# Blockwise causal attention and a gated FFN on one core: moving the casting loads of batches 4 to 7, and batch 3's key and query copies, within the order of issue

## The chip, the cores and the metric
One core of a Trainium2 chip runs the whole program as one launch. The metric is the device time of an execution in microseconds (us). PE, ACT, DVE, POOL and SP are the core's engines: matmul, activation, vector, GpSimd and the engine that issues most transfers. A line of the form "L266" is line 266 of the kernel file.

## The reference
The input is q, k and v of 8 batches, 8 heads, 576 positions and 64 dimensions in float32, and three weights. Cut to what matters:

```python
scores = (q @ k.T) / sqrt(64)                   # per batch and head
scores = where(pos_q // 64 >= pos_k // 64, scores, -1e9)
attn   = softmax(scores)                        # float32
x      = (attn @ v) -> [4608 tokens, 512]       # heads side by side
out    = (relu(x @ w_gate) * (x @ w_val)) @ w_out   # 512 -> 1536 -> 512
```

## The kernel before, in words
**Tiles.** The FFN works on nine tiles j of 512 tokens. Tile j, for j from 0 to 7, holds the first 512 positions of batch j; the ninth tile holds the last 64 positions of all eight batches. One tile is 144 matmuls: 12 blocks f of d_ff, each four for the gate and four for the value (L615), and then four output blocks of 12 (L634). `ffn_gen` yields after each of them, so the kernel counts in *places*: place p of a tile is its p-th FFN matmul, and places 0 to 95 are gate and value, 96 to 143 the outputs.

**Attention between the FFN matmuls.** While tile b-1 runs, the attention of batch b is laid between its matmuls: four rounds r = 4b to 4b+3, one for each pair of heads hp = 0 to 3, and one "tail" for the last 64 queries. A round begins with `visit` (L426, scores from `kTm` and `qTm` of its hp), goes on with exponentials on ACT (L435, L441), zeroed corners on DVE (L495), two `head_av` (L553, then L507 and L508 on DVE, which write `xnat`), and ends with `to_xT_dma` (L583), a transposing transfer issued by SP that writes one quarter of `xT`, the operand of FFN tile b. Tile b can't run the fourth matmul of its first block before the fourth quarter of its `xT` has landed. The tail is `tail_visit` (L460, reads `kTm`, all hp), `tail_av` (L522, reads `v_bf`) and L536.

**Order.** The order on every engine is written by hand: `run(base, events)` sorts (place, function) pairs and calls each function after so many FFN matmuls. Each engine goes through its own list in that order and waits there only for the data and buffers of the next instruction. So a place fixes what stands before what on an engine; a transfer whose inputs and buffer are free may be issued long before the FFN reaches that place.

**How q, k and v come in.** Batches 0 to 3 are loaded as float32 into `stage` by SP and cast on POOL or DVE. For batches 2 and 3 the main parts of q and k are transposed by SP into `perm` (L252, one transfer for each of q and k and half hg = hp // 2), and `unpermute` puts them in order: for each hp a copy of 128x512 into `qTm` on DVE and one into `kTm` on POOL, both L266. `v_3` casts batch 3's v on POOL (L203, L217); it writes `v_bf` of the batches with odd number and so waits for the tail of batch 1. Batches 4 to 7 are loaded by `load_qkv` (L316), transfers that POOL issues and that cast on the way: five for each of q, k and v. SP then transposes q and k straight into `qTm`, `kTm`, `qTt`, `kTt` (`dma_transposes`, L326 and L330). All buffers `qTm`, `kTm`, `qTt`, `kTt`, `v_bf`, and `q_bf`, `k_bf`, exist twice, for even and odd batches. So v of batch b+1 can only be loaded once the tail of batch b-1 is through, and q and k of batch b+2 only once those of batch b have been transposed.

**Around the change.** Tile 1 (base 144) runs batch 2, tile 2 (base 288, `b == 3` in the last loop) runs batch 3 with its rounds 12 to 15 at places 2, 26, 74 and 96, and the tail of batch 2 at places 50, 69 and 73. Written `un(3, hp, (dve, pool))`, batch 3's copies stand at place 124 of tile 1 (hp 0) and places 11, 35 and 83 of tile 2 (hp 1 to 3); the loads of q and k of batch 4 stand at place 1 of tile 2.

```python
264  def unpermute(self, hp, engs):
265      for t in range(2):
266          engs[t]((qTm, kTm)[t]..., self.perm[t, hp // 2]...)
304  def load_qkv(b, which):
305      for t in which:
307          for c in range(NCH):          # NCH = 5
316              nc.gpsimd.dma_start(dst, src...)
```

Of the kernel before, what the change touches and what calls it, by code (L numbers as in the profile page):

```python
# [17 lines left out]
def kernel(  # L18
# [12 lines left out]
    B, H, S, D = q.shape  # L31
# [78 lines left out]
    def new_bf():  # L110
        return [sb.tile([128, 2048], BF, name=n, bufs=2) for n in ("q_bf", "k_bf")]

    def new_bt():
        return [sb.tile([64, 512], BF, name=n, bufs=2) for n in ("q_bt", "k_bt")]
# [189 lines left out]
    def load_qkv(b, which):  # L304
        for t in which:
            src = (q, k, v)[t]
            for c in range(NCH):
                n = 128 if c < 4 else 64
                if t == 2:
                    dst = v_bf[b % 2][:n, c, :, 0:64]  # L310
                else:
                    if (b, 0) not in bfs:
                        bfs[b, 0], bfs[b, 1] = new_bf(), new_bt()
                    dst = bfs[b, 0][t][:, 512 * c : 512 * c + 512] if c < 4 else bfs[b, 1][t]
                    dst = dst.rearrange("p (h d) -> p h d", h=8)
                nc.gpsimd.dma_start(  # L316
                    dst,
                    src[b, :, 128 * c : 128 * c + n, :].rearrange("h p d -> p h d"),
                )
# [3 lines left out]
    def dma_transposes(b):  # L323
        m, tl = bfs[b, 0], bfs[b, 1]
        for t in range(2):
            nc.sync.dma_start_transpose(  # L326
                (qTm, kTm)[t][b % 2].rearrange("p c h n -> p (c h) n"),
                m[t],
            )
            nc.sync.dma_start_transpose((qTt, kTt)[t][b % 2][:, 0:4, :], tl[t])  # L330
# [337 lines left out]
    dve, act, pool = nc.vector.tensor_copy, nc.scalar.copy, nc.gpsimd.tensor_copy  # L668
    with tc.manual_schedule(engines={E.PE, E.DVE, E.Activation, E.Pool, E.SP}):
# [89 lines left out]
        def run(base, events):  # L759
            for p, f in sorted(events, key=lambda e: e[0]):  # L760
                upto(base + p)
                f()

        def round_at(p, r, av, to_xT, late=(), corner_eng=None):

            exps = []

            def begin():
                exps.extend(visit(r))
                exps[0]()  # L770
                exps[1]()

            return [
                (p, begin),
                (p + 6, lambda: exps[2]()),
                (p + 13, lambda: corners(r, corner_eng or nc.vector)),
                (av[0], lambda: head_av(r, 0)),
                (av[1], lambda: head_av(r, 1)),
                (to_xT[0], lambda: to_xT[1](r)),
            ]  # L780

        def tail_at(p, b, av):
            exps = []
            x = sb.tile([64, 512], BF, name="xtail", bufs=2)

            def begin():
                exps.extend(tail_visit(b))
                exps[0]()
                exps[1]()

            def end():
                tail_av(b, 1, x)
                tail_to_xT(b, x)

            return [
                (p, begin),
                (p + 6, lambda: exps[2]()),
                (av[0], lambda: tail_av(b, 0, x)),
                (av[1], end),
            ]  # L800
# [53 lines left out]
        def un(b, hp, engs=(dve, dve)):  # L854
            return lambda: early[b].unpermute(hp, engs)

        events = []
# [12 lines left out]
        events = tail_at(4, 0, (20, 24)) + tail_at(116, 1, (132, 136))  # L870
        for r, p in ((8, 32), (9, 52), (10, 72), (11, 92)):
# [12 lines left out]
            (82, lambda: mains_3(4)),  # L884
            (101, lambda: early[3].transpose(1)),
            (118, lambda: early[3].transpose_tails()),
            (124, un(3, 0, (dve, pool))),
            (137, v_3),
        ]
        run(144, events)  # L890
        for b in range(3, B):
            events = tail_at(120, b, (136, 140))
            if b == 3:
                events += tail_at(50, 2, (69, 73))
                events.append((1, lambda: load_qkv(4, (0, 1))))
            for i, p in enumerate((2, 26, 74, 96) if b == 3 else (2, 32, 62, 92)):
                r = 4 * b + i
                events += round_at(p, r, (p + 20, p + 24), (p + 24, to_xT_dma))
                if b == 3 and i < 3:
                    events.append((p + 9, un(3, i + 1, (dve, pool))))  # L900
            if b + 1 < B:
                events.append((75 if b == 3 else 28, lambda b=b: load_qkv(b + 1, (2,))))
                events.append((60, lambda b=b: dma_transposes(b + 1)))
            if b + 2 < B:
                events.append((100 if b == 3 else 59, lambda b=b: load_qkv(b + 2, (0, 1))))
            run(144 * (b - 1), events)
        ffn(10**6)
        store.pop()()
# [28 lines left out]
```

## Time and profile before
| | |
|---|---|
| median of 11 runs | 380.26 us (377.51 to 383.24) |
| the profiled execution's own time | 376.65 us |
| its span, first to last instruction | 374.9 us |
| outside the span | 1.75 us |
| PE busy | 358.7 us, 96% of the span |
| DVE, ACT, POOL busy | 169.2, 171.2, 118.9 us |
| granted TensorE clock | 1.000 |
| moved by POOL's casting loads | 8.13 MB, 56576 packets |

The span is what the views of the profile divide. PE is not busy for 16.2 us of it. The windows view gives PE's busy time for each stretch of the span; the waits view says what PE waited for; the timeline of POOL says what was issued ahead of it.

### The profile page before, as it was taken

The numbers are of one execution on the slowest core, as the hardware profiler recorded it, in microseconds if no ns is written. First come the engines' busy times: TensorE is split into PE (matmuls) and PEld (weight loads), VectorE is DVE, ScalarE is ACT, GpSimd is POOL, SyncE is SP. The second block draws the span as 40 slices with busy tenths as digits, with TensorE's granted clock in tenths as the row PEclk, the third lists the DMA queues.
The fourth block names the chain that finished last, engine by engine and source line by source line (L and its number), as shares of the span: only waits on it lengthen the run. The fifth ranks groups of instructions, "written<-read, shape, count | busy, mean of one in ns | idle before, by whom it ended". The sixth has DMA issues, their size and how long they took to land.

```text
span 374.9 us, 7560 instructions
## 1 busy us (share of the span) xinstructions
PE 358.7 (96%) x3004; PEld 177.3 (47%) x3004; DVE 169.2 (45%) x392; ACT 171.2 (46%) x283; POOL 118.9 (32%) x156
## 2 busy tenths in 40 slices
PE   7898979999996999899999999999999999999995
PEld 2644444544553545454554455444544454444443
DVE  3644455556543564355335552554345444323432
ACT  4923744576533563455545534653366423302310
POOL 5678767346167086480058003000000000000000
PEclk9999999999999999999999999999999999999999
DMA  8999999969989299999689965945200130020014
GB/s 255 293 370 356 373 185 297 205 170 246 189 129 124 56 126 145 172 130 146 152 95 131 123 125 95 62 79 135 77 16 17 42 100 7 2 84 28 3 35 105
DMA packets 140739, 51.35 MB, mean 137 GB/s; under 512 B 120352, under 2 KB 133920, under 8 KB 140704
## 3 DMA queue, kind: packets, MB, share of 16 engines
q0 software_dynamic: 56576, 8.13, 43.2%
q1 hardware_dynamic: 79424, 34.62, 42.3%
q10 hardware_dynamic: 4704, 8.13, 6.6%
q8 instruction: 23, 0.38, 0.4%
q14 instruction: 12, 0.10, 0.1%
HBM read 37.75 MB, written 9.44 MB: 126 GB/s over the span
## 4 chain that ended last, share of the span: by engine, by line
PE 64%; DMA 2%; DVE 1%; POOL 1%; ACT 0%; issue 0%
PE ffnp L615 36%; PE ffnp L634 18%; PE ffnp L553 3%; DMA xT<-xnat 2%; PE sc L426 2%; PE ffnp L522 2%; PE one L426 1%; PE sc L460 1%; DVE hT L628 0%; PE one L460 0%; POOL kTm L266 0%; POOL k_bf L316 0%; DVE qTm L266 0%; POOL k_bt L316 0%; ACT gate_sb L624 0%
## 5 line engine op out<-in xcount | busy, mean ns | idle before, releaser
L628 DVE TENSOR_TENSOR hT<-gate_sb,ffnp 128x512 bf16<-128x512 bf16 x108 | 74.2, 687 | 100.8 <-PE ffnp L615 80.5
L624 ACT ACTIVATE gate_sb<-ffnp 128x512 bf16<-128x512 f32 x108 | 65.0, 602 | 101.6 <-PE ffnp L615 101.5
L615 PE MATMUL ffnp<-xT,wg 128*128 128x512 bf16 x384 | 102.1, 379 | 1.1 <-DMA xT<-xnat 1.1
L615 PE MATMUL ffnp<-xT,wv 128*128 128x512 bf16 x384 | 102.1, 379 | 0.3 <-ACT gate_sb L624 0.2
L634 PE MATMUL ffnp<-wo,hT 128*128 128x512 bf16 (+1 forms) x444 | 102.3, 373 | 0.0
L615 PEld LDWEIGHTS <-wv 128*128 128x128 bf16 x432 | 40.1, 98 | 47.4 <-issue 4.1
L615 PEld LDWEIGHTS <-wg 128*128 128x128 bf16 x432 | 40.0, 98 | 46.5 <-issue 3.2
L634 PEld LDWEIGHTS <-hT 128*128 128x128 bf16 x444 | 40.2, 98 | 40.0 <-issue 0.8
L435 ACT ACTIVATE attnT<-sc 128x1024 bf16<-128x1024 f32 x56 | 56.9, 1040 | 0.0
L644 DVE COPY ob<-ffnp 128x512 f32<-128x512 f32 (+1 forms) x37 | 25.1, 677 | 41.1 <-PE ffnp L634 41.1
L316 POOL DMA_DIRECT2D v_bf<-in_v_dram x20 | 16.8, 856 | 66.7 <-PE ffnp L522 51.7
L553 PEld LDWEIGHTS <-attnT 128*128 128x128 bf16 x640 | 26.3, 98 | 15.1 <-DVE xnat L508 4.4
L507 DVE RECIPROCAL recip<-ffnp 128x4 f32<-128x4 f32 (+1 forms) x76 | 13.6, 179 | 36.8 <-PE ffnp L553 26.4
L441 ACT ACTIVATE attnT<-one 128x256 bf16<-128x256 f32 x28 | 10.7, 383 | 38.9 <-PE ffnp L426 26.8
L553 PE MATMUL ffnp<-v_bf,attnT 128*128 128x65 bf16 x600 | 28.2, 194 | 0.1
L508 DVE TENSOR_TENSOR xnat<-ffnp,recip 128x256 bf16<-128x256 f32 x60 | 25.5, 424 | 2.1
L426 PEld LDWEIGHTS <-kTm 64*128 64x128 bf16 x224 | 8.7, 94 | 18.4 <-issue 10.6
L426 PE MATMUL sc<-qTm,kTm 64*128 64x512 bf16 (+1 forms) x168 | 16.7, 305 | 0.0
L481 ACT ACTIVATE attnTt<-one 64x256 bf16<-64x256 f32 x8 | 3.0, 376 | 28.0 <-PE ffnp L460 28.0
L472 ACT ACTIVATE attnTt<-sc 128x1024 bf16<-128x1024 f32 x16 | 15.6, 1015 | 0.0
L316 POOL DMA_DIRECT2D k_bf<-in_k_dram x16 | 14.1, 896 | 3.2 <-DMA v_bf<-in_v_dram 3.2
L316 POOL DMA_DIRECT2D q_bf<-in_q_dram x16 | 14.4, 923 | 1.5 <-DMA k_bf<-in_k_dram 1.5
(88 smaller groups left out, 261.1 us busy)
## 6 DMA issues: line engine op xcount, KB each, us to landing
out_dram<-ob ACTq DMA_DIRECT2D x28, 256.0 KB, 2.3
stage<-in_moe_w_gate_dram SPq DMA_DIRECT2D x6, 512.0 KB, 9.3
stage<-in_moe_w_val_dram SPq DMA_DIRECT2D x6, 512.0 KB, 9.5
stage<-in_q_dram SPq DMA_DIRECT2D x6, 512.0 KB, 7.0
stage<-in_k_dram SPq DMA_DIRECT2D x6, 512.0 KB, 7.9
stage<-in_moe_w_out_dram SPq DMA_DIRECT2D x6, 512.0 KB, 9.2
stage<-in_v_dram SPq DMA_DIRECT2D x8, 256.0 KB, 7.1
q_bf<-in_q_dram POOLq DMA_DIRECT2D x16, 128.0 KB, 6.4
```

Source lines behind the costliest of these rows:

```text
L316: nc.gpsimd.dma_start(dst, src[b, :, 128 * c : 128 * c + n, :].rearrange("h p d -> p h d"),)
L426: nc.tensor.matmul(where[c].rearrange("p (c n) -> p c n", n=128), kTm[b % 2][head_of(hh), c, hp, :], qTm[b % 2][head_of(hh), c:4, hp, :], ...
L435: return lambda: nc.scalar.activation(at[:, :, lo : lo + 512], sc, AF.Exp, scale=scale)
L472: return lambda: nc.scalar.activation(at[:, :, 2 * i : 2 * i + 2, 0:256], main[i].rearrange("p g (h n) -> p g h n", h=2), AF.Exp, scale=scale,
L507: nc.vector.reciprocal(recip, av[:, :, 64])
L508: nc.vector.tensor_tensor(out=out, in0=av[:, :, 0:64], in1=recip.to_broadcast([rows, n, 64]), op=AX.mult,)
L553: nc.tensor.matmul(av[:, p, :], at[:, hh, col : col + 128], vb[:, c, h, :], start=(p == 0), stop=(c == p), skip_group_check=True,)
L615: nc.tensor.matmul((gate, val)[t], (wg, wv)[t][i][:, c, fo : fo + 128], x[:, c], start=(c == 0), stop=(c == 3),)
L624: nc.scalar.activation(gate_sb, gate, AF.Relu)
L628: nc.vector.tensor_tensor(out=h, in0=gate_sb, in1=val, op=AX.mult)
L634: nc.tensor.matmul(op, hT[f][:, 128 * s : 128 * (s + 1)], wo[f // 4][:, f % 4, n0:n1], start=(f == 0), stop=(f == 11),)
L644: nc.vector.tensor_copy(ob, op)
```

## The change
- `un(3, 0)` moves from place 124 to 121 of tile 1, and `un(3, 1)` from place 11 of tile 2 to place 125 of tile 1, so both stand ahead of `v_3` (place 137).
- `un(3, 2)` moves from place 35 to place 3 of tile 2, and `un(3, 3)` from place 83 to place 33.
- `load_qkv` of q and k: for batch 4 from place 1 to place 4 of tile 2, so behind `un(3, 2)`. For batch 5 from place 100 of tile 2 to place 4 of tile 3; for batches 6 and 7 from place 59 of the tile before to place 4 of the tile in which the batch before them runs.
- `load_qkv` of v: from place 28 to place 46 for batches 5 to 7; it stays at place 75 for batch 4.
- `dma_transposes` moves from place 60 to 66 in every tile.

```diff
-            (124, un(3, 0, (dve, pool))),
+            (121, un(3, 0, (dve, pool))),
+            (125, un(3, 1, (dve, pool))),
             (137, v_3),
         ]
         run(144, events)
...
             events = tail_at(120, b, (136, 140))
             if b == 3:
                 events += tail_at(50, 2, (69, 73))
-                events.append((1, lambda: load_qkv(4, (0, 1))))
             for i, p in enumerate((2, 26, 74, 96) if b == 3 else (2, 32, 62, 92)):
                 r = 4 * b + i
                 events += round_at(p, r, (p + 20, p + 24), (p + 24, to_xT_dma))
-                if b == 3 and i < 3:
-                    events.append((p + 9, un(3, i + 1, (dve, pool))))
+            if b == 3:
+                events.append((3, un(3, 2, (dve, pool))))
+                events.append((33, un(3, 3, (dve, pool))))
             if b + 1 < B:
-                events.append((75 if b == 3 else 28, lambda b=b: load_qkv(b + 1, (2,))))
-                events.append((60, lambda b=b: dma_transposes(b + 1)))
-            if b + 2 < B:
-                events.append((100 if b == 3 else 59, lambda b=b: load_qkv(b + 2, (0, 1))))
+                for at, which in ((4, (0, 1)), (75 if b == 3 else 46, (2,))):
+                    events.append((at, lambda b=b, w=which: load_qkv(b + 1, w)))
+                events.append((66, lambda b=b: dma_transposes(b + 1)))
             run(144 * (b - 1), events)
```

## The prediction
> **What bounds the kernel now.** I read the page's head, then PE's waits, then the windows of 10 us, then the timelines of POOL, PE and DVE where PE stands still, and last the chain at the tile boundary.
>
> ```profile
> span 374.9 us, 7560 instructions
> PE 358.7 (96%) x3004; PEld 177.3 (47%) x3004; DVE 169.2 (45%) x392; ACT 171.2 (46%) x283; POOL 118.9 (32%) x156
> ...
> PE one L426 <- POOL kTm L266: 3.5, 1, 3.5
> ...
> PE ffnp L615 <- DMA xT<-xnat: 1.1, 1, 1.1
> ...
> 110.00:120.00 10.00, 6.53 (x53) 3.17 (x52) 3.99 (x10) 3.93 (x8) 9.70 (x11) 1.00 2.04 113
> 120.00:130.00 10.00, 10.00 (x102) 5.07 (x100) 5.38 (x12) 6.75 (x11) 0.00 (x0) 1.00 0.59 46
> 130.00:140.00 10.00, 9.90 (x108) 5.09 (x106) 5.73 (x13) 5.77 (x11) 7.22 (x9) 1.00 1.80 143
> ...
> 150.00:160.00 10.00, 8.90 (x82) 4.45 (x79) 3.74 (x10) 4.28 (x7) 4.91 (x6) 1.00 2.00 170
> ```
>
> PE is busy for 96% of the span. After 60 us the windows (busy PE is the second number) show only three holes: 3.47 us in 110 to 120, 0.10 in 130 to 140 and 1.10 in 150 to 160; all others are at 9.96 or more. The first is one single wait of PE for a key copy on POOL, the third one wait for the last quarter of an `xT`. Of the other 11.5 us of idle PE, 7.6 lie before 60 us and 3.9 behind the last matmul, where the change moves nothing. Now what stood on POOL ahead of that key copy (start, duration, instruction, idle time before it and what ended that):
>
> ```profile
> 100.37 1.08 POOL L266 COPY kTm<-perm 128x512 bf16<-128x512 bf16 x1 [9.36 <-PE sc L460]
> 106.50 2.03 POOL L203 CAST v_bf<-stage 128x1024 bf16<-128x1024 f32 x2 [5.05 <-PE ffnp L522]
> 108.47 0.61 POOL L217 CAST v_bf<-stage 64x512 bf16<-64x512 f32 x1
> 109.03 3.75 POOL L316 DMA_DIRECT2D q_bf<-in_q_dram  x4
> ...
> 116.91 0.75 POOL L316 DMA_DIRECT2D k_bt<-in_k_dram  x1
> 117.59 2.11 POOL L266 COPY kTm<-perm 128x512 bf16<-128x512 bf16 x2
> 132.78 4.19 POOL L316 DMA_DIRECT2D v_bf<-in_v_dram  x5 [13.08 <-issue]
> 136.93 1.11 POOL L266 COPY kTm<-perm 128x512 bf16<-128x512 bf16 x1
> 137.94 3.54 POOL L316 DMA_DIRECT2D q_bf<-in_q_dram  x4
> ```
>
> And PE at that time:
>
> ```profile
> 114.80 0.48 PE L553 MATMUL ffnp<-v_bf,attnT 128*128 128x65 bf16 x10
> 118.76 0.28 PE L426 MATMUL one<-qTm,kTm 64*128 64x256 bf16 x1 [3.47 <-POOL kTm L266]
> ```
>
> Batch 3's v casts end at 109.1, then POOL issues the ten loads of q4 and k4 (109.03 to 117.66, 8.6 us), and only then the key copy of hp 1 (117.6 to 118.7). Round 13, at place 26, wanted it when PE was through at 115.29. It got it at 118.76. The copy's own inputs had long been there: its `perm` was written for hp 0 as well, which was copied at 100.37.
>
> **The change part by part.** The instruction orders of the two programs are the same on PE, ACT and SP; they differ on POOL and DVE only in where batch 3's eight copies stand.
>
> *Key copies on POOL.* New order: hp 0, hp 1, v casts, hp 2, q4/k4, hp 3, v4, q5/k5. With the durations above: hp 0 at 100.37 to 101.45; hp 1 at 101.45 to 102.5 (its buffer is freed by the same tail scores, L460, as that of hp 0); the v casts still wait for L522 and run from 106.50 to 109.08, since 4 us of POOL's 5.05 us wait are left over; hp 2 from 109.08 to 110.15; q4/k4 from 110.15 to 118.8; hp 3 to 119.9. Round 13 finds its keys 12.8 us early. PE's 3.47 us go.
>
> *What is late next at round 13.* Besides keys, round 13 needs banks of PSUM. Its second piece (the "ffnp" one) takes one that DVE frees: by 115.34 block 2's product (L628, 114.66 + 0.68) and by 114.74 the first `xnat` of round 12 are through; PE gets there at 115.29 + 0.12 = 115.41. Its first big piece needs the exponential L435 that ended at 110.57. So at most 0.1 us takes the place of the wait. If PE's tail were paced by DVE's second `xnat` instead (115.54 + 0.42 = 115.96), 0.55 us would be left; I take 0 and keep 0.55.
>
> *Query copies on DVE.* The same four copies of 0.59 to 0.60 us move to places where DVE is idle: hp 0 and hp 1 at 102.5 to 103.7 (next on DVE is an `ob` copy at 104.49), hp 2 at about 109.0 (DVE then idles until 111.09, waiting for ACT's gate), hp 3 into the slot that hp 2 had at 121.84, which opens 3.47 us earlier. The `perm` transfers for hp 2 and 3 are issued by SP at 99.32 and 100.68 and these transfers took 3.2 to 4.8 us to land, so by 105.5: 3.5 us before either copy. What leaves is this:
>
> ```profile
> 121.84 0.59 DVE L266 COPY qTm<-perm 128x512 bf16<-128x512 bf16 x1
> ...
> 135.53 1.06 DVE L266 COPY qTm<-perm 128x512 bf16<-128x512 bf16 x1
> 137.01 0.69 DVE L628 TENSOR_TENSOR hT<-gate_sb,ffnp 128x512 bf16<-128x512 bf16 x1
> ```
>
> The copy at 135.53, beside POOL's v4 loads, took 1.06 us, held up the next product, and PE's hole of 0.10 us before 137.75 follows from it. In the new order hp 3 lands beside the k4 loads (118.4), so the long form and the 0.10 us may just move there: 0 to 0.1 gained, I take 0.
>
> [...] The change puts DVE's and POOL's copies of hp 2 side by side at 109.05, and one query copy among k4's loads. The rows say less: POOL's 32 wide q and k load issues took 876 to 1102 ns, also those beside the DVE copy at 111.70 (0.60 us); of four query copies beside POOL work one was longer, by 0.46 us, and beside another a cast on POOL took 1.46 us where its like took 1.04. By the rows the price is 0 to 0.46 us on either engine. [...]
>
> *Loads of batch 4.* 1.1 us later on POOL, one key copy in front. In before they landed 3.3 to 6.5 us after issue; k4's last is now issued at about 118.8 and lands by 125.3. SP's transposes of k4 come at 132.70 - 3.47 = 129.2, those of q4 at 124.8 with q landed by about 121. Cost 0; with 6 us less cover SP would pass the delay to the `xT` quarters behind.
>
> *Loads of batches 5 to 7 and the transposes.* Their places in the text move by up to 90, but on POOL everything from v4 on has the same neighbours (v4, q5/k5, v5, q6/k6, ...), except hp 3's copy, and the same buffers to wait for. v5's first issue at 152.23 waited for tail 3's L522, v6's and v7's for 22.6 and 25.9 us for the same line: POOL runs ahead up to a buffer, and the place doesn't hold it. SP's order is unchanged too. So "none in the last third of a tile" doesn't come about in time: q5/k5 are still issued as soon as v4 is. Cost 0, gain 0.
>
> *The next boundary.* Where the 3.47 us could be lost again:
>
> ```profile
> 146.55 0.43 DVE xnat L508
> 147.00 8.14 DMA xT<-xnat
> 155.18 4.26 PE ffnp L615 x19
> ```
>
> The last quarter of `xT` for tile 3 takes 8.14 us to land, against 2.4 to 2.6 us for transposes in quiet stretches (126.9, 209, 224), because it runs among q5/k5 (k5's issues took 11.9 to 13.5 us to land). PE wants it at 154.08 and waits 1.10. All here hangs on PE: tail 2's L522 releases v4, v4 is followed by q5/k5, round 15 releases the transpose. So it all shifts by 3.47 us, and as hp 3's copy no longer stands between v4 and q5, q5/k5 start up to 1.0 us earlier relative to it. [...] The rows speak for less: k5's issues waited for v4's loads to land (0.88 and 0.84 us of idle POOL at 143.5 and 145.2), and that landing isn't moved. Between 0 and 1.0 I take 0.4.
>
> *Sum against the profiled execution.* 3.47 + 0 + 0.4 = 3.87 us: span 374.9 to 371.0, time 376.65 to 372.8. That execution is 3.6 us below the median of the runs shown, below the fastest even; the wait removed comes from POOL's order alone, not from a landing, so I carry it over unchanged: 380.26 - 3.87 = 376.4. The unknowns give 2.9 (0.55 left at round 13, nothing at the boundary) to 4.6 (1.0 and 0.1 more): 375.7 to 377.4. A measurement of this kernel can tell about 0.5%, 1.9 us, from no change.
>
> **The rivals.**
> - *The boundary eats it (same).* If the transfers from 128 to 155 us are a fixed amount of work at a full rate that doesn't begin earlier, the last `xT` quarter lands at 155.1 whenever it is issued, PE waits up to 1.10 + 3.47 us there, and the time stays at 380.3; half of that gives 378.5. For it: landings of 8 to 13.5 us. Against: 120 to 130 us moved only 46 GB/s, POOL stood idle for 13.08 us until v4 was released by PE. The stretch starts on PE's signal.
> - *Batch 5's loads catch the transpose (slower).* Starting 1.0 us earlier they may stand wholly in front of round 15's transpose instead of partly behind it. Its landing decides: up to 8.14 + 3.47 = 11.6 us there is still a gain. At 13.5 us, the longest landing of a k5 load, PE loses 5.4 more: 380.26 + 1.9 = 382.2. Against: the longest landing of any `xT` transpose there is 9.6 us (round 14).
> - *The executions differ from the profile (faster still).* With 3.6 us between profile and median, there may be a longer wait at the same place in most runs, up to 3.6 more: 372.8 to 375.7.
> - *It doesn't do what it says.* For the loads of batches 5 to 7 that is my forecast already; for the key copies it can't be, as their order on POOL does change.
>
> **How the numbers follow.** Forecast 0.74 (375.7 to 377.4), faster still 0.05, boundary 0.13 (378.0 to 380.5; a fifth of it still over 0.5% faster), slower 0.08 (over 380.5; a quarter of it within 0.5%). That makes faster 0.79 + 0.03 = 0.82; I take off 0.03 as the median itself moves by about 1 us from set to set: 0.79. Same 0.14, slower 0.07. The range reaches from 374.0, half of the faster rest, to 379.6, most of the boundary case.
>
> **What would show it.** Right: no wait of PE for `kTm` L266; window 110 to 120 full; POOL with two key copies before the v casts and one on either side of the q4/k4 loads; L426 of round 13 at about 115.3; the loads from v4 on at their old distance from PE's tail scores; a wait at tile 3's first block between 0.1 and 1.1 us. Wrong: that wait at 3 us or more (boundary), landings of over 11.6 us (slower), PE waiting at round 13 for DVE, or q6/k6 issued only when PE reaches tile 4, which would mean that places do hold POOL.

## The result and the profile after

The changed kernel takes 373.72 us (median of 12, 371.61 to 377.72), against 379.46 us for the kernel before (47 runs in all). The ratio is 0.9858, 95% interval 0.9831 to 0.9886: about 5.4 us, 4.3 to 6.4 by the interval. Comparisons and the means further down leave out executions more than 1.5% above the fastest of the same kernel in their set of runs. The forecast was 376.4 us in a range of 374.0 to 379.6, from a gain of 3.87 us. It started from a median before of 380.26 us, and from there the ratio gives 374.9 us; the measured median itself lies 0.3 us below the range. Faster was right; the gain is about 1.5 us larger than the sum, and the experiments look for these 1.5 us.

The profiled execution after has almost the span of the one before. The page's head, PE's waits and the windows of 10 us (the second number is busy PE, the last three are the granted clock, that is the share of its full clock that PE was given, the transfers' share and GB/s):

```profile
span 374.5 us, 7561 instructions
...
PE ffnp L615 <- DMA xT<-xnat: 1.6, 1, 1.6
...
10.00:20.00 10.00, 7.86 (x116) 5.57 (x114) 6.05 (x17) 7.62 (x12) 5.90 (x16) 0.83 1.03 293
...
50.00:60.00 10.00, 9.45 (x86) 4.75 (x87) 3.20 (x9) 5.16 (x9) 7.39 (x11) 0.83 1.03 252
...
110.00:120.00 10.00, 10.00 (x73) 4.71 (x72) 5.74 (x11) 5.80 (x11) 10.00 (x13) 1.00 1.12 76
120.00:130.00 10.00, 9.90 (x114) 5.30 (x113) 5.46 (x12) 6.38 (x11) 2.48 (x3) 1.00 1.22 101
...
150.00:160.00 10.00, 8.44 (x70) 4.06 (x68) 3.70 (x11) 4.28 (x7) 4.72 (x6) 1.00 2.25 164
```

No wait for a key copy is left among PE's waits, and 110 to 120 us is full. But twice before 60 us, where nothing was changed, the clock fell (0.83 over 10 us), and round 12 starts at 111.29 us instead of 108.62. So two spans compare badly; stages compare well. Here is POOL's list and PE's rounds 12 to 15 and the next boundary, all of after:

```profile
103.04 2.10 POOL L266 COPY kTm<-perm 128x512 bf16<-128x512 bf16 x2 [12.29 <-PE sc L460]
109.18 2.03 POOL L203 CAST v_bf<-stage 128x1024 bf16<-128x1024 f32 x2 [4.03 <-PE ffnp L522]
...
111.71 1.06 POOL L266 COPY kTm<-perm 128x512 bf16<-128x512 bf16 x1
112.72 3.64 POOL L316 DMA_DIRECT2D q_bf<-in_q_dram  x4
...
120.47 0.77 POOL L316 DMA_DIRECT2D k_bt<-in_k_dram  x1
121.15 1.33 POOL L266 COPY kTm<-perm 128x512 bf16<-128x512 bf16 x1
132.22 4.19 POOL L316 DMA_DIRECT2D v_bf<-in_v_dram  x5 [9.74 <-issue]
136.37 3.55 POOL L316 DMA_DIRECT2D q_bf<-in_q_dram  x4
```

```profile
111.29 0.28 PE L426 MATMUL one<-qTm,kTm 64*128 64x256 bf16 x1
...
117.89 0.28 PE L426 MATMUL one<-qTm,kTm 64*128 64x256 bf16 x1
...
131.96 0.28 PE L426 MATMUL one<-qTm,kTm 64*128 64x256 bf16 x1
...
137.76 0.28 PE L426 MATMUL one<-qTm,kTm 64*128 64x256 bf16 x1
...
154.83 0.38 PE L615 MATMUL ffnp<-xT,wg 128*128 128x512 bf16 x1 [1.56 <-DMA xT<-xnat]
```

POOL's order is the forecast one. From such first matmuls of the rounds, each stage's length in us (the third column is a later profile of the same changed kernel):

| stage | before | after | after, again |
|---|---|---|---|
| round 12 to 13 | 10.14 | 6.60 | 6.60 |
| round 13 to 14 | 13.75 | 14.07 | 14.06 |
| round 14 to 15 | 6.07 | 5.80 | 5.81 |
| round 15 to 16 | 14.47 | 14.47 | 14.47 |
| round 16 to the end of the span | 221.85 | 222.27 | 221.43 |
| sum | 266.28 | 263.21 | 262.37 |

The wait of 3.5 us is gone in full and the stages behind it gain or lose a few tenths. In all that is 3.1 to 3.9 us, which fits the forecast sum but not the 5.4 us of the times.

### The profile page after: what moved, and what is told of

Its sections match the earlier page's. It is cut to its first block, busy times and chain, and to the rows that moved or that the text cites. A ratio compares the mean times of both kernels' runs of the same rounds, so it can differ in the third digit from the quotient of the medians.

```text
span 374.5 us, 7561 instructions
## 1 busy us (share of the span) xinstructions
PE 360.6 (96%) x3004; PEld 179.0 (48%) x3004; DVE 172.4 (46%) x392; ACT 171.4 (46%) x283; POOL 118.2 (32%) x156
## 4 chain that ended last, share of the span: by engine, by line
PE 88%; DMA 7%; DVE 1%; POOL 1%; issue 1%; SPq 1%; ACT 0%; DVEq 0%; POOLq 0%
PE ffnp L615 49%; PE ffnp L634 24%; PE ffnp L553 5%; PE sc L426 3%; DMA stage<-in_k_dram 3%; DMA xT<-xnat 2%; PE ffnp L522 2%; DMA stage<-in_q_dram 2%; PE one L426 1%; PE sc L460 1%; SPq L132 1%; DVE hT L628 1%; PE ffnp L281 1%; PE ffnp L573 1%; PE sc L375 0%
```

## The experiments

**The parts of the change apart.** First, the copies alone; every load stays at its old place:

```diff
-            (124, un(3, 0, (dve, pool))),
+            (121, un(3, 0, (dve, pool))),
+            (125, un(3, 1, (dve, pool))),
...
-                events.append((1, lambda: load_qkv(4, (0, 1))))
+                events.append((4, lambda: load_qkv(4, (0, 1))))
+                events.append((3, un(3, 2, (dve, pool))))
+                events.append((33, un(3, 3, (dve, pool))))
...
-                if b == 3 and i < 3:
-                    events.append((p + 9, un(3, i + 1, (dve, pool))))
```

> Before with batch 3's eight copies moved as in the change, and every load and transpose left at its old place. If a place in the text doesn't hold POOL (the forecast), this gives the whole of the change: 0.9858, that is about 5.4 us off, like the changed kernel. If the loads' new places carry the part of the gain that the forecast's sum (3.9 us) lacks, about 1.5 us are missing here: 0.990. In the trace: no wait of PE for a key copy of round 13, and POOL's loads of v5, q6/k6 and later at the same distance from PE's tails as in the changed kernel.

Measured: 374.74 us, ratio 0.9874 (0.982 to 0.9929). The copies are the whole change, within the interval.

Second, the loads and transposes alone:

```diff
-                events.append((1, lambda: load_qkv(4, (0, 1))))
...
             if b + 1 < B:
-                events.append((75 if b == 3 else 28, lambda b=b: load_qkv(b + 1, (2,))))
-                events.append((60, lambda b=b: dma_transposes(b + 1)))
-            if b + 2 < B:
-                events.append((100 if b == 3 else 59, lambda b=b: load_qkv(b + 2, (0, 1))))
+                for at, which in ((4, (0, 1)), (75 if b == 3 else 46, (2,))):
+                    events.append((at, lambda b=b, w=which: load_qkv(b + 1, w)))
+                events.append((66, lambda b=b: dma_transposes(b + 1)))
```

> Before with only the loads and the transposes at their new places, the copies left at theirs. Forecast: nothing, ratio 1.000 within 0.3%, PE still waits 3.5 us for the key copy at round 13, and the tile boundary behind round 15 is as before (PE waits about 1.1 us for the last quarter of xT). Rival, that spreading the loads is what pays: 1.5 to 5 us off, 0.987 to 0.996, and q5/k5 issued at least 5 us later against PE's tail 3.

Measured: 378.03 us, ratio 0.9984 (0.9947 to 1.0021). No effect, as forecast: the places don't hold POOL, and the distance of the loads to PE's tails is the same before and after (ahead of v6, POOL waits 22.6 us for L522 in both profiles). In this profile q6/k6 stay where they were, far ahead of tile 4's FFN: POOL is through with them by 170 us and idle from there to 190. But the same trace showed what the profile of before had not. The windows view, 2 us each:

```profile
116.00:118.00 2.00, 0.00 (x0) 0.00 (x0) 0.28 (x1) 0.00 (x0) 2.00 (x4) 1.00 2.13 140
118.00:120.00 2.00, 0.92 (x10) 0.46 (x11) 0.00 (x0) 0.54 (x3) 2.00 (x2) 0.99 3.30 147
120.00:122.00 2.00, 2.00 (x6) 0.70 (x5) 0.00 (x0) 2.00 (x4) 0.02 (x1) 0.50 2.94 96
122.00:124.00 2.00, 2.00 (x7) 0.76 (x6) 1.50 (x4) 0.65 (x2) 0.00 (x0) 0.66 0.12 7
124.00:126.00 2.00, 2.00 (x18) 1.04 (x17) 0.69 (x1) 0.87 (x2) 0.00 (x0) 1.00 0.00 0
```

PE's wait ends at 119.08. About 1 us later the granted clock is 0.50 for some 3.4 us. PE is shown busy, but its matmuls take longer: four FFN matmuls there last 1.91 us, against 1.03 us at the same place in the profile of before. Round 13 to 14 took 15.44 us here, against 13.75: 1.69 us more, 0.45% of the span. So the wait can cost more than its own length. This gives the clock theory, which the next experiments test: the missing 1.5 us is this stretch, which most executions of before have behind round 13 and the profiled one happened not to have.

Third, hp 1's copies alone (hp 2 stays behind q4/k4, hp 3 behind v4):

```diff
             (124, un(3, 0, (dve, pool))),
+            (125, un(3, 1, (dve, pool))),
...
-                if b == 3 and i < 3:
+                if b == 3 and i in (1, 2):
```

> Before with one copy pair moved, that of hp 1 (ahead of the v casts); hp 2 stays behind the q4/k4 loads, hp 3 behind the v4 loads. If round 13's wait is all of it: 3.5 us off at least, and as much as the whole change, 0.986. If in most executions round 15's key copy behind v4 is late too (in the profile of before it ended 0.54 us before its use), or if hp 3's copy ahead of q5/k5 costs at the boundary, part is missing: 3.5 us only, 0.991, and the trace shows PE waiting for kTm at round 15 or the hole of 0.1 us there, or a longer wait at tile 3's first block.

Measured: 374.18 us, ratio 0.9856 (0.9804 to 0.9908): as much as the whole change. Hp 2's and hp 3's copies do nothing that could be measured, and the idea that hp 3's place costs at round 15 or at the boundary has no support in the times. The only profile is of an execution of 381.27 us; no time is read from it. But it shows the boundary and the clock once more (PE's wait, then windows of 1 us):

```profile
PE ffnp L615 <- DMA xT<-xnat: 3.5, 2, 2.0
...
158.00:159.00 1.00, 0.85 (x3) 0.29 (x3) 0.00 (x0) 0.17 (x1) 0.71 (x1) 0.52 2.45 192
159.00:160.00 1.00, 1.00 (x4) 0.40 (x3) 0.00 (x0) 1.00 (x2) 0.64 (x1) 0.50 1.99 102
```

Here the last quarter of `xT` took 10.6 us to land, and PE stood still for 2.01 and 1.45 us with one matmul between, until 158.15. From 158.0 to 160, where these windows end, the clock is 0.50 to 0.52. So the half clock also follows idle PE at another place, with no late key. Why the landing was so long is not shown.

**The clock theory.** The wait kept, but filled: 14 matmuls in front of round 13, whose result nobody reads.

```diff
                 r = 4 * b + i
+                if b == 3 and i == 1:
+                    events.append((p, lambda: junk(14)))
                 events += round_at(p, r, (p + 20, p + 24), (p + 24, to_xT_dma))
```

> Before, with 14 matmuls of 128x512 into an unused bank put on PE right in front of round 13 (they work on v's copy, nothing reads their result): PE is busy for about 3.0 of the 3.5 us in which it waits for hp 1's key copy, and the wait itself stays. Clock theory (the wait of 3.5 us is often followed by a stretch of about 3.4 us at half the granted clock, as the trace of the loads-only kernel shows once, worth 1.7 us): the mean granted clock of the runs rises from about 0.991 to 0.995, as with the changed kernel, and 1.0 to 1.7 us come off, ratio 0.9955 to 0.997. Theory of the sum alone (the wait costs 3.5 us and nothing else): ratio 1.000 or a little above, clock as before.

Measured: 376.61 us, ratio 0.9951 (0.9916 to 0.9986). PE's timeline and the windows:

```profile
115.45 3.18 PE L664 MATMUL ffnp<-v_p,ident 128*128 128x512 bf16 x14
118.83 0.28 PE L426 MATMUL one<-qTm,kTm 64*128 64x256 bf16 x1 [0.20 <-POOL kTm L266]
...
118.00:120.00 2.00, 1.80 (x14) 0.70 (x13) 0.00 (x0) 0.80 (x3) 1.77 (x2) 1.00 2.66 131
120.00:122.00 2.00, 2.00 (x11) 0.90 (x10) 0.70 (x2) 2.00 (x3) 0.00 (x0) 1.00 1.53 99
```

Round 13 starts as late as before (10.16 us after round 12), work was only added, and the kernel is faster by 0.5 to 3.2 us. The sum alone can't give that. The mean granted clock of its runs is 0.9956, against 0.9914 for before in the same set. The idle PE is the cause, not the late key.

The wait shortened: two k4 loads go behind hp 1's key copy.

```diff
-    def load_qkv(b, which):
+    def load_qkv(b, which, cs=range(NCH)):
...
-                events.append((1, lambda: load_qkv(4, (0, 1))))
+                events.append((1, lambda: load_qkv(4, (0,))))
+                events.append((1, lambda: load_qkv(4, (1,), range(3))))
+                events.append((12, lambda: load_qkv(4, (1,), range(3, NCH))))
```

> Before with the last two k4 loads (0.87 and 0.69 us of POOL) moved behind hp 1's key copy: the wait at round 13 shrinks from 3.5 to about 1.9 us. Sum alone: 1.6 us off, ratio 0.996. Clock theory: a wait that short doesn't bring the clock down, so the half-clock stretch goes too: 2.6 to 3.3 us off, ratio 0.991 to 0.993, and the runs' mean granted clock is that of the changed kernel, about 0.995.

Measured: 376.20 us, ratio 0.994 (0.9904 to 0.9977), 2.3 us off by the ratio. That lies between the two forecasts, and the interval holds both. The clock theory's expectation was wrong in one thing: in the profiled execution the shorter wait did bring the clock down:

```profile
117.38 0.28 PE L426 MATMUL one<-qTm,kTm 64*128 64x256 bf16 x1 [1.92 <-POOL kTm L266]
...
118.00:120.00 2.00, 2.00 (x9) 0.73 (x6) 0.00 (x0) 2.00 (x5) 1.87 (x3) 0.50 2.20 149
120.00:122.00 2.00, 2.00 (x8) 0.75 (x7) 0.98 (x2) 0.76 (x1) 0.00 (x0) 0.69 1.50 92
```

So 1.92 us of idle PE can be enough, though on the mean (below) these runs lose no more by the clock than those without a wait.

The wait restored in the changed kernel, and longer, as hp 2's copy stays ahead of q4/k4:

```diff
-            (125, un(3, 1, (dve, pool))),
...
                 events.append((3, un(3, 2, (dve, pool))))
+                events.append((5, un(3, 1, (dve, pool))))
```

> The changed kernel with hp 1's copies put back behind the q4/k4 loads (hp 2 stays ahead of them): PE waits for the key copy at round 13 for 3.5 us plus the 1.05 us of hp 2's copy, about 4.5 us. Sum alone: 4.5 us above the changed kernel, 378.2 us, ratio to before 0.997. Clock theory: such a wait brings the half-clock stretch in nearly every execution, 1.5 to 1.7 us more: 379.8 us, ratio 1.000 to 1.002, and a mean granted clock of about 0.990. If something else in the change carried the gain, the time stays near 374.

Measured: 380.49 us, ratio 1.0049 (1.001 to 1.0088): 6.8 us above the changed kernel by the medians, for a wait of 4.38 us. The sum alone (0.997) lies outside the interval; the clock theory's 1.000 to 1.002 reaches just into it and was itself too low.

```profile
121.95 0.28 PE L426 MATMUL one<-qTm,kTm 64*128 64x256 bf16 x1 [4.38 <-POOL kTm L266]
...
122.00:124.00 2.00, 2.00 (x12) 0.75 (x13) 0.00 (x0) 1.67 (x4) 0.89 (x1) 0.61 2.38 150
124.00:126.00 2.00, 2.00 (x7) 0.73 (x6) 0.46 (x1) 1.31 (x2) 0.00 (x0) 0.53 0.02 1
```

**All runs by their clock.** Every execution has a mean granted clock. Span times (1 - clock) is what it lost by a lower clock, and one stretch of 3.4 us at half clock is 1.7 us of it. A mean clock says how much an execution lost, not where; where is seen in profiles alone. Means over the executions compared (for the runs of before in the first comparison no clock is on record):

| PE at round 13 | executions | mean clock | lost, us | of them under 0.9925 |
|---|---|---|---|---|
| waits 3.5 us (before, three sets) | 50 | 0.9910 | 3.40 | 32 |
| waits 3.5 us (loads only) | 10 | 0.9922 | 2.94 | 4 |
| waits 3.5 us (v of batch 5 first, in before; see below) | 12 | 0.9933 | 2.51 | 7 |
| waits 4.4 us (hp 1 put back) | 10 | 0.9901 | 3.75 | 8 |
| waits 1.9 us (wait halved) | 12 | 0.9953 | 1.75 | 1 |
| filled with matmuls | 12 | 0.9956 | 1.66 | 0 |
| no wait (the change, copies only, again) | 22 | 0.9952 | 1.78 | 1 |
| no wait (hp 1 only) | 5 | 0.9966 | 1.27 | 0 |
| no wait (v of batch 5 first, twice; see below) | 12 | 0.9958 | 1.58 | 0 |

Before loses 3.40 - 1.78 = 1.6 us more than the changed kernel, about one stretch per execution on the mean. With the 3.5 us of the wait that is 5.1 us; measured were 5.4 (4.3 to 6.4). The size is not a constant. In its three sets before loses 2.88, 3.24 and 4.43 us; kernels of the same sets without the idle stretch lose 1.27 to 1.71, 1.66 and 1.86, so 1.2 to 2.6 us less. The two other kernels that wait 3.5 us lose only 1.2 and 0.7 us more than the changed one.

What the kernels without a wait still lose comes from the unchanged start and, where it costs nothing, from the stretch behind PE's last matmul: in the five profiles of kernels with the change's copies and no wait, no low clock lies anywhere else. Among the four profiles with a wait of 3.5 us or more at round 13, three have the low clock right behind it; the profile of before is the fourth.

**The boundary.** V of batch 5 ahead of its q and k, in the changed kernel:

```diff
-                for at, which in ((4, (0, 1)), (75 if b == 3 else 46, (2,))):
+                for at, which in ((5 if b == 4 else 4, (0, 1)), ({3: 75, 4: 4}.get(b, 46), (2,))):
```

> The changed kernel with v of batch 5 issued ahead of q and k of batch 5. v5 waits on POOL for PE's tail 3, so q5/k5 can't be under way when round 15's transpose runs. If the transpose's 8 us come from the q5/k5 loads in flight: it lands in 2.4 to 5 us, PE's wait of 1.1 to 1.6 us at tile 3's first block goes, and the time falls by that against the changed kernel: ratio to before about 0.982. If it is slow because of the v4 loads or of the transposes before it, the landing stays near 8 us and the time at 0.986. Slower (up to 2 us) if q5/k5, now about 20 us later, hold up SP's transposes of batch 5 and with them the quarters of the next xT.

Measured: 371.89 us, ratio 0.9819 (0.977 to 0.9867). POOL's timeline and, last, the time to landing of round 15's transpose:

```profile
148.75 4.23 POOL L316 DMA_DIRECT2D v_bf<-in_v_dram  x5 [15.00 <-issue]
152.94 3.54 POOL L316 DMA_DIRECT2D q_bf<-in_q_dram  x4
...
DMA to landing us min/median/max: 2.4/2.4/2.4
```

With q5/k5 not yet issued, the transpose lands in 2.4 us instead of 7.4 to 8.6 (10.6 in the profile of hp 1's copies alone), and PE doesn't wait. The same edit in before:

```diff
-                events.append((75 if b == 3 else 28, lambda b=b: load_qkv(b + 1, (2,))))
+                events.append(({3: 75, 4: 4}.get(b, 28), lambda b=b: load_qkv(b + 1, (2,))))
...
-                events.append((100 if b == 3 else 59, lambda b=b: load_qkv(b + 2, (0, 1))))
+                if b > 3:
+                    events.append((59, lambda b=b: load_qkv(b + 2, (0, 1))))
+            if b == 4:
+                events.append((5, lambda: load_qkv(5, (0, 1))))
```

> Before with v of batch 5 issued ahead of q and k of batch 5, and the copies untouched: the wait at round 13 stays, the one at tile 3's first block should go, as in the changed kernel with the same edit, which was 1.8 us below the changed kernel. If the boundary cost before more than it does after the change (the share of the gain that the sum lacks): 3 us or more off, ratio 0.992 or below. If it cost the same: 1 to 2 us, 0.995 to 0.997.

Measured: 377.74 us, ratio 0.9979 (0.9939 to 1.002). About 0.8 us off, not separable from nothing, less than the 1 to 2 us of an unchanged cost, and not the 0.992 that would have made the boundary the source of the missing 1.5 us. PE doesn't wait at tile 3's first block here either. The profile has the half clock behind round 13's wait once more:

```profile
118.64 0.28 PE L426 MATMUL one<-qTm,kTm 64*128 64x256 bf16 x1 [3.48 <-POOL kTm L266]
...
120.00:122.00 2.00, 2.00 (x7) 0.71 (x6) 0.59 (x1) 2.00 (x3) 0.00 (x0) 0.52 1.76 103
122.00:124.00 2.00, 2.00 (x7) 0.75 (x6) 0.91 (x4) 0.60 (x1) 0.00 (x0) 0.63 0.01 1
```

**Both once more in one set.** The changed kernel, unedited:

> The changed kernel once more, beside the next one on the same chip. Clock theory: the runs' mean granted clock is again near 0.995 (before: 0.990), and the ratio to before near 0.986. If the 5.4 us of the first comparison were a matter of the set of runs and the wait alone is worth its 3.5 us: 0.990, and a mean clock no higher than that of before.

Measured: 373.82 us, ratio 0.9847 (0.9816 to 0.9878), clocks of 0.993 to 0.998. The first comparison holds, and so does the clock theory's forecast: a mean clock of 0.995, against 0.988 for before in this set. And v of batch 5 first, the edit shown above:

> The changed kernel with v of batch 5 ahead of q and k of batch 5, once more, to compare with the changed kernel within one set. Its first set was at 371.9 us. If the wait for the last quarter of xT is what it takes away (0.6 to 1.6 us in the traces of the kernels with the changed order): 1 to 2 us below the changed kernel, ratio to before 0.981 to 0.984, no wait at tile 3's first block, and the transpose of round 15 landing in about 2.4 us again. If the first set was a favourable one: level with the changed kernel.

Measured: 374.07 us, ratio 0.9845 (0.9807 to 0.9882): level with the changed kernel here, where the first set had it ahead. By the traces the edit works both times: the landing is 2.5 us again, and from round 15 to the end of the span the two profiles need 235.0 us, against 235.7, 235.9 and 236.7 for the changed order. A gain of 0.7 to 1.7 us is there in the stage; the start, which varies by more than that (round 12 begins between 108.6 and 112.1 us in these profiles), hides it. Over both sets the mean is 372.75 us (12), against 373.66 for the changed kernel (22). That it beats the changed kernel is shown in this stage of the two traces, not settled in the times.

## Why the prediction was right, and where its sum fell short

- *Key copies on POOL, 3.47 us.* Right. The stage from round 12 to 13 lost 3.54 us, and POOL runs in the order and with the waits that were worked out (4.03 us left ahead of the v casts, 4.0 forecast).
- *What is late next at round 13.* Taken as 0; its second piece starts 0.18 us behind the first, so about 0.1 us. Round 13 to 14 is 0.3 us longer; part of it is a hole of 0.10 us at 125 us, ahead of `head_av`. Round 14 to 15 is 0.3 us shorter, as hp 3's slow query copy is no longer in it (it is 6.1 us in all profiles with that copy there, 5.8 in all others). The two cancel, as the forecast's 0 had it.
- *Query copies on DVE.* Right that PE pays nothing; the 0 to 0.46 us read from the rows was too little. The two copies of hp 2 did run side by side, and DVE's took 1.66 us instead of 0.59, longer by about POOL's 1.06, while POOL's own kept its 1.06. DVE's row begins first, at 111.58 against POOL's 111.71; why it is the longer one is not shown. A load issue beside a query copy took as long as before: the k4 issue beside hp 3's copy took 0.77 us, before 0.75. DVE's idle time ahead of the first product took it up: that product starts 2.48 us after round 12, before 2.47.

```profile
111.58 1.66 DVE L266 COPY qTm<-perm 128x512 bf16<-128x512 bf16 x1
113.77 0.69 DVE L628 TENSOR_TENSOR hT<-gate_sb,ffnp 128x512 bf16<-128x512 bf16 x1 [0.53 <-ACT gate_sb L624]
```

- *Loads of batches 4 to 7.* Right: nothing (0.9984).
- *The next boundary, 0.4 us gained.* Not seen. The wait there is 1.6, 0.6 and 0.7 us in three profiles of the changed order, 1.1, 0 and 1.2 in three of the order before. It is a scatter about which one profile says little. No run shows the 0.4 us: in after q5/k5 do start 1.0 us closer behind v4 (4.15 us after its first issue, before 5.16), but k5's first issue stands no closer (10.88, before 10.70), and round 15's transpose took 8.6, 7.6 and 7.7 us to land in the same three profiles of the changed order, against 8.1 in the profile of before.
- *Carrying the sum over to the median.* This is the step that failed: "the wait removed comes from POOL's order alone, not from a landing, so I carry it over unchanged". The wait has indeed the same length in every trace, but not the same price. In three of four profiles PE comes out of it at half clock, and on the mean of the runs that costs about 1.6 us, a term that the sum put at nothing. The profile of before, with a clock of 1.000, was an exception, and the 3.6 us between it and the median were a hint at what else the executions had in them. The measured time lies outside the forecast's main case (375.7 to 377.4) and inside that of the rival "the executions differ from the profile" (372.8 to 375.7). This rival named the place and its size, but guessed a longer wait. It got 0.05, so the wide range, and not the main case, caught the result.

## What to carry to other kernels

An idle stretch of a busy matmul engine can cost its length plus a slow stretch behind it: here 3.5 us cost about 5.1 on the mean. Look up the granted clock in more than one execution before a profile at full clock is taken for the rule. Where a late input can't be had earlier, matmuls that nobody reads may keep the clock, and gave about a third of the gain here (0.49% of 1.42%, at a mean clock of 0.9956 against 0.9914). In a list that an engine works through in order, a small copy that a busy engine waits for belongs ahead of a block of transfer issues; where in the text the transfers themselves stand is worth nothing if a buffer, and not the list, holds them (here a ratio of 0.9984, 0.9947 to 1.0021).

## What the hardware showed

- Behind the waits at round 13 the half clock begins 0.4 to 1.4 us after the wait's end, in four profiles, and lasts about 3.4 us. Three of four waits of 3.5 to 4.4 us had it behind them, and so did the one of 1.92 us that was profiled. Counted back 3.4 us, the length of a stretch, from where the low clock begins, PE was idle for 1.9 to 3.0 us in these four profiles and in that of hp 1's copies alone. In the profile of before it was idle for 3.47 us on end, and the clock stayed at 1.00. So how much idle PE it takes is not shown.
- Round 15's transpose, in flight among the ten casting loads of q5 and k5, needs 7.4 to 8.6 us to land in seven profiles (10.6 in one more), without them 2.4 to 2.5 in two profiles.
